# Two block sums of a weight matrix moved from VectorE to GpSimd, with two smaller moves beside them

## The chip, the cores and the metric

The kernel runs on one core of a Trainium2 chip. A core has five engines, each with its own instruction stream: TensorE (PE in the profile, with PEld for its weight loads), VectorE (DVE), ScalarE (ACT), GpSimd (POOL) and SyncE (SP), which here issues most of the DMAs. The engines run side by side and wait for each other through semaphores; each works through its own instructions in the order written. TensorE writes its results into PSUM, from where VectorE or ScalarE has to take them; POOL works on SBUF only in this kernel.

The metric is the device time of one execution in microseconds (us), the median of several runs. Lower is better.

## The reference

For each of 8 batches and 8 heads there is an `x` of 512 rows by 64 and a `state` of 32 rows by 64. Two attentions read from each other, and the rows of both results, with the heads side by side, pass through two layers with a leaky rectifier between them:

```python
scores = scale * np.matmul(x, state.transpose(0, 1, 3, 2))   # softmax over the 32 states -> a
xread = np.matmul(a, state)
scores2 = scale * np.matmul(state, x.transpose(0, 1, 3, 2))  # softmax over the 512 rows -> a2
sread = np.matmul(a2, x)
# rows of xread and sread of a batch: 512 + 32, each of 8 * 64 = 512 columns
h = x @ w_in                  # 512 -> 2048
g = np.maximum(0.01 * h, h)
out = g @ w_out               # 2048 -> 512
```

The output has 8 * 544 = 4352 rows of 512 float32.

## The kernel before, in words

**The first layer** of a batch isn't taken from `xread`. The kernel multiplies the batch's state by `w_in` first (`a_m`, matmuls of line 411, result `pm` in PSUM, copied to the tile `M`), and then `M` by the transposed softmax `aT` (`ff1`, line 432): two matmuls for each of 16 tiles of 128 hidden columns. ScalarE takes each result from PSUM through the rectifier into `hT` (line 437). Two PSUM banks of the tag "ph" take turns, so a tile's matmuls need the eviction of the tile two before it.

**The second layer** of batch 0 is written out in plain form (`piece`, line 537): four row tiles `i` of 128 rows, each 16 matmuls against the rows of `w_out_bf`, then a copy from PSUM into `ysb` and a store (`y_store`, lines 547 and 548). Row tiles 2 and 3 of batch 0 lie in one double PSUM bank, `wide` (`pyw` in the profile), with the tag "big"; tiles 0 and 1 in banks of the tag "py". The next user of "big" in TensorE's order is the `a_m` of batch 1's last quarter of `w_in`, in the step s = 3 of batch 1's first layer; it needs both copies out of `pyw`.

From batch 1's second half on, the second layer is made with seven block products instead of eight (a Winograd form). It needs four block sums of the weights, made once: `tw_sum(n, ...)`, line 576, with n = 1 to 4. Each is 8 row tiles by 256 columns:

```python
1: lambda: (w_block(0, 1, j0, j1), w_block(0, 0, j0, j1)),
2: lambda: (w_block(1, 1, j0, j1), tw[1][u][:, at]),
3: lambda: (w_block(1, 1, j0, j1), w_block(0, 1, j0, j1)),
4: lambda: (w_block(1, 0, j0, j1), tw[2][u][:, at]),
```

(first minus second in each; the fourth needs the second, the second needs the first). It also needs four block sums of `hT` for each batch: `s_sum` (line 597, tiles `S1` to `S4`) for whole batches, and `two_sum` (line 673, tiles `Sr`) for the second half of batch 1, whose state is `q1`. `two_product` (line 689, PSUM `ppr`) and `product` (line 632, `ppx` and `ppb`) are the matmuls of the seven products; product 7 uses the third block sum of the weights, product 4 the fourth, 5 and 6 the first and second. The additions of line 699 put two products together into `ysb` and free a PSUM bank.

**The order of work is written by hand.** All engines are scheduled manually: an engine does its instructions in the order in which the Python code issues them. Around the change this order is:

- a stretch ahead of batch 1's first layer (lines 992 to 1049): softmax of batch 1, the casts of x[2] and the cast of the states (`state_cast`, line 209, on POOL), the rest of batch 0's second layer, then `tw_sum(2)` on VectorE in two halves, `a_probs2(a0)` (two tiny operations, lines 345 and 347, and two scalings of 128x512, line 355, that finish batch 0's second softmax), `tw_sum(3)` on VectorE, and `cast_all(3)`, POOL's cast of x[3] to bfloat16 (line 132);
- batch 1's first layer (lines 1053 to 1095), s = 0 to 15. At s = 1 and 3 the last matmuls of batch 0's row tiles and their copies are issued; at s = 3 the scores of batch 2 (`a_scores(a2)`, line 256), the `a_m` into "big", and on VectorE `a_shift(a2)` (row maxima, line 266; spread, line 274; subtraction, line 280) and `a_max2` (line 331); ScalarE's exponential (line 284) follows at s = 7; at s = 9 VectorE makes the reciprocal and `aT` (lines 289 to 302) and `tw_sum(4)`;
- batch 2's first layer (line 1115 on), with the seven products of `q1` between its steps. At s = 0 VectorE makes the second halves (j = 4 to 7) of the sums 1 and 2 of `q1`, at s = 1, behind the shift of batch 3, the second half of sum 3; POOL makes sum 4, casts the other states and x[4].

SyncE's queue holds, in this order around the change: the load of x[3], four stores of batch 0's rows, eight small loads of states (line 203), the transpose of batch 3's x (line 234), which needs POOL's cast of x[3], then the transposes of the second softmaxes of batches 0 and 1.

Of the kernel before, what the change touches and what calls it, by code (L numbers as in the profile page):

```python
# [27 lines left out]
def kernel(  # L28
# [9 lines left out]
    nc = tc.nc  # L38
# [14 lines left out]
    VEC, SCA, POO = nc.vector.tensor_copy, nc.scalar.copy, nc.gpsimd.tensor_copy  # L53
# [261 lines left out]
    def a_shift(a):  # L315
        a_max(a)
        a_diff(a)

    def a_exp(a):
        a.e1 = block_exp(a.sh, NB)  # L320
# [230 lines left out]
    HJ = 8  # L551
# [12 lines left out]
    def w_block(r, c, j0, j1):  # L564
        return w_out_bf[:, HJ * r + j0:HJ * r + j1, HN * c:HN * (c + 1)]

    def tw_sum(n, j0, j1, eng):
        u, at = j0 // 4, slice(j0 % 4, j0 % 4 + j1 - j0)
        in0, in1 = {
# [4 lines that stand above are left out]
        }[n]()  # L574
        with nc.allow_low_precision(reason="operands of bf16 products"):
            eng.tensor_tensor(out=tw[n][u][:, at], in0=in0, in1=in1, op=ALU.subtract)  # L576
# [467 lines left out]
    for j in (0, 4):  # L1044
        tw_sum(2, j, j + 4, nc.vector)
    a_probs2(a0)
    for j in (0, 4):
        tw_sum(3, j, j + 4, nc.vector)
    cast_all(3)


# [3 lines left out]
    for s in range(16):  # L1055
        ff1(a1, h1, s)
        if s in (1, 3):
            two = ((2, SCA), (3, VEC)) if s == 1 else ((0, VEC), (1, SCA))
            for i, copy in two:
                piece(0, h0, i, 3, copy=None, js=half[1])  # L1060
            for i, copy in two:
                y_store(0, i, copy)
        elif s % 2:
            piece(*fill[s // 2 - 2])
        if s == 3:
            a_scores(a2)
            m_evict(a1, 3, a_m(a1, 3, "big"), SCA)
            a_shift(a2)
            a_max2(a2)
        elif s == 5:  # L1070
            load_state(1)
        elif s == 7:
            a_exp(a2)
            a_open(att_of[3], 3)
            a_xt_dma(att_of[3])
        elif s in (9, 11):
            a_exp2(a2, s // 2 - 4)
            if s == 9:
                a_a2t_pair(0, (0,))
                a_recip(a2)  # L1080
                a_probs(a2)
                for j in (0, 4):
                    tw_sum(4, j, j + 4, nc.vector)
            else:
                a_probs2(a2)
                load_x(4, nc.sync)
        elif s == 13:
            a_probs2(a1)
            a_a2t_pair(0, (1,))
            pm = [a_m(a2, 0, "big"), a_m(a2, 1, "sc")]  # L1090
            m_evict(a2, 0, pm[0], SCA)
            m_evict(a2, 1, pm[1], VEC)
            q1 = two_open(h1, 2 * P, ("S0", "S1"), "py")
            for n in (1, 2, 3):
                two_sum(q1, n, 0, 4, nc.vector)

# [16 lines left out]
    for b in range(2, B):  # L1115
        hT = hpool.tile([P, 16, S], BF16, name="hT", tag="hT")
        hTs[b] = hT
        a = att_of[b]
        nxt = att_of[b + 1] if b + 1 < B else None
        if b == 2:  # L1120
            two_keep(q1, "S2")
            fill = {i: [lambda i=i: piece(1, h1, i, 3)] for i in range(2)}
            for s, n in zip((2, 3, 5, 6, 8, 9, 11), (1, 2, 6, 5, 3, 7, 4)):
                fill[s] = [lambda n=n: two_product(q1, n)]
            fill[11].append(lambda: nc.sync.dma_start(pair_rows(1, 1), q1.y[:]))
        else:
            order = (2, 6, 5, 7, 3, 4)
            fill = {
                s: [lambda n=order[s // 2], v=s % 2: product(b - 1, n, v)] for s in range(12)
            }  # L1130
            for i, n in enumerate(order):
                if n not in (2, 7):
                    fill[2 * i + 1].append(lambda n=n: after(b - 1, n))
        fill[12 if b < 6 else 13] = [lambda: product(b, 1, 0)]
        fill[14] = [lambda: product(b, 1, 1, 0, 4)]
        fill[15] = [lambda: product(b, 1, 1, 4, 8), lambda: after(b, 1)]
        mid = MID.get(b, ())
        for s in range(16):
            ff1(a, hT, s)
            if mid and s == (1 if b == 2 else 2):  # L1140
                (o, c, tag), (o2, c2, tag2) = mid
                pm = a_m(att_of[o], c, tag)
                a_scores(nxt)
                m_spread(o2, c2, a_m(att_of[o2], c2, tag2))
                m_evict(att_of[o], c, pm, SCA)
                a_shift(nxt)
                if b > 2:
                    a_max2(nxt)
                else:
                    two_sum(q1, 3, 4, 8, nc.vector)  # L1150
            if s == 0:
                if b + 2 < B:
                    open_xb(b + 2)
                if b == 7:
                    a_a2t_pair(6)
                elif b != 6:
                    a_a2t(a)
                for n in (1, 2):
                    if b > 2:
                        s_sum(b - 1, n, 4, 8, nc.vector)  # L1160
                    else:
                        two_sum(q1, n, 4, 8, nc.vector)
            elif s == 1:
                if b > 2:
                    for j in range(0, HJ, 2):
                        s_sum(b - 1, 4, j, j + 2, nc.gpsimd)
                else:
                    for j in (4, 0):
                        two_sum(q1, 4, j, j + 4, nc.gpsimd)
                    state_cast(1, nc.gpsimd)  # L1170
                if b + 2 < B:
                    cast_all(b + 2)
            elif s == 4:
                if b == 2:
                    state_t(1)
                    a_sread(a0)
            elif s == 7:
                if b == 2:
                    a_sread(a1)
            elif s == 13:  # L1180
                if b < 6:
                    a_sread(a)
            elif s == 10:
                if b == 7:
                    a_sread(att_of[6])
            elif s == 12:
                if b == 7:
                    a_sread(a)
                for n in (1, 2):
                    s_sum(b, n, 0, 4, nc.vector)  # L1190
                for j in (0, 4):
                    s_sum(b, 3, j, j + 4, nc.vector)
            if nxt is not None:
                if s == 4 + bool(mid):
                    a_exp(nxt)
                elif s in ((6, 9) if b == 2 else (6, 7)):
                    if b == 2 and s == 6:
                        for f in fill.pop(6):
                            f()
                    a_exp2(nxt, int(s > 6))  # L1200
                if s == 7:
                    a_recip(nxt)
            if s == 9 and b + 2 < B:
                a_open(att_of[b + 2], b + 2)
                a_xt_dma(att_of[b + 2])
                if b + 3 < B:
                    load_x(b + 3, nc.sync)
            if b == 7:
                if s == 0:
                    fa_open()  # L1210
                elif s == 13:
                    fb_sums()
            for f in fill.get(s, ()):
                f()
            if b == 7 and s in FA_AT:
                i = FA_AT.index(s)
                fa_sum(i % 4 + 1, FJ * (i // 4), FJ * (i // 4 + 1))
            if s == 1:
                if b > 2:
                    after(b - 1, 2)  # L1220
            elif s == 3 and b == 2:
                a_max2(nxt)
            elif s == 7 and b > 2:
                after(b - 1, 7)
            if nxt is not None:
                if s == (8 if b == 2 else 7):
                    a_probs(nxt)
                elif s == 9:
                    a_probs2(nxt)
                elif s == 10:  # L1230
                    pms = [a_m(att_of[o], c, t) for o, c, t in END.get(b, ())]
                    for (o, c, t), pm in zip(END.get(b, ()), pms):
                        if t == "phpy":
                            m_spread(o, c, pm)
                        else:
                            m_evict(att_of[o], c, pm, VEC if t == "big" else SCA)
# [76 lines left out]
```

## Time and profile before

| | us |
|---|---|
| median of 3 runs (204.12 to 204.14) | 204.12 |
| the profiled execution | 203.73 |
| its span, first to last instruction | 202.0 |
| TensorE busy (matmuls) | 195.7 |
| VectorE busy | 162.1 |
| ScalarE busy | 141.8 |
| GpSimd busy | 63.4 |
| VectorE busy from 40 to 50 us | 9.67 |
| VectorE busy from 50 to 60 us | 9.79 |

In the timelines a line is: start, length, engine, line of the kernel, operation, output and inputs by the program's names, their shapes, and the number of instructions merged into it (x4). In brackets stands how long the engine was idle before and what it waited for. Start and length of a merged line are from its first start to its last end. The length of one VectorE or ScalarE instruction includes a tail in which the next one already runs: 0.69 us sums follow each other at 0.60. The ends of matmuls are modelled; the distance between their starts is the better measure: two matmuls of 512 columns take 0.43 us. The granted clock of TensorE is full in the whole profile.

### The profile page before, as it was taken

What the parts mean: (1) busy time and instruction counts of PE and PEld (TensorE: products, weight loads), DVE (VectorE), ACT (ScalarE), POOL (GpSimd) and SP (SyncE); (2) the same over time, 40 slices, a digit from 0 to 9 for tenths busy, and PEclk for the clock granted to TensorE, in tenths of its full rate; (3) what the DMA queues carried; (4) which work ended last, traced back from release to release, by engine and by line L of the source; (5) the groups of instructions that cost most, each with busy time, mean ns of one, the idle gap of its engine ahead of it and who ended that gap; (6) DMA issues with size and microseconds to landing.
All of it is one profiled execution on the core that took longest, in us unless ns stands there. A gap on an engine that the chain in (4) does not pass through costs nothing.

```text
span 202.0 us, 4620 instructions
## 1 busy us (share of the span) xinstructions
PE 195.7 (97%) x1880; PEld 130.0 (64%) x1880; DVE 162.1 (80%) x245; ACT 141.8 (70%) x272; POOL 63.4 (31%) x68
## 2 busy tenths in 40 slices
PE   7899999999989999999999999999999999999993
PEld 3643544444457667776776767676767777799982
DVE  2666797999999989974998889897999945984712
ACT  3679647889888868866787779686868555757420
POOL 8914181030280175017400670054004600540000
PEclk9999999999999999999999999999999999999999
DMA  5999999797999622953382505220025302210115
GB/s 197 212 207 298 209 290 154 165 344 151 246 219 200 229 52 43 247 229 60 61 248 109 159 3 104 105 107 0 0 86 166 63 3 97 114 43 12 52 40 170
DMA packets 38773, 27.75 MB, mean 137 GB/s; under 512 B 24416, under 2 KB 35808, under 8 KB 38752
## 3 DMA queue, kind: packets, MB, share of 16 engines
q1 hardware_dynamic: 33584, 20.78, 38.4%
q0 software_dynamic: 4832, 6.29, 15.3%
q10 hardware_dynamic: 336, 0.39, 0.7%
q8 instruction: 14, 0.23, 0.5%
q14 instruction: 7, 0.06, 0.1%
HBM read 17.30 MB, written 8.91 MB: 130 GB/s over the span
## 4 chain that ended last, share of the span: by engine, by line
PE 67%; DMA 15%; DVE 11%; POOL 3%; issue 1%; ACT 1%; ACTq 1%; POOLq 0%; DVEq 0%
PE ph L432 19%; PE ppx L632 18%; PE ppb L632 15%; DMA w_out_bf<-in_moe_w_out_dram 7%; DMA x<-in_x_dram 7%; PE ppr L689 5%; PE pf L510 3%; PE pm L411 3%; PE ppw L632 3%; DVE Sr L673 2%; POOL w_in_bf L145 2%; PE psr L384 2%; DVE tw L576 2%; DVE sh L274 1%; DVE mrow L266 1%
## 5 line engine op out<-in xcount | busy, mean ns | idle before, releaser
L437 ACT ACTIVATE hT<-ph 128x512 bf16<-128x512 f32 x112 | 66.6, 604 | 25.2 <-PE ph L432 24.3
L432 PE MATMUL ph<-aT,M 128*128 128x512 bf16 x224 | 65.3, 380 | 0.1
L597 POOL TENSOR_TENSOR S<-hT,S 128x512 bf16<-128x512 bf16 x24 | 31.9, 1348 | 84.5 <-DVE S L597 58.1
L632 PEld LDWEIGHTS <-S 128*128 128x128 bf16 x384 | 37.0, 98 | 12.7 <-issue 0.9
L632 PEld LDWEIGHTS <-hT 128*128 128x128 bf16 x288 | 28.0, 98 | 11.1
L597 DVE TENSOR_TENSOR S<-hT 128x1024 bf16<-128x1024 bf16 x24 | 24.1, 1031 | 4.4 <-ACT hT L437 4.4
L432 PEld LDWEIGHTS <-M 128*128 128x128 bf16 x224 | 20.9, 98 | 8.9 <-issue 3.0
L632 PE MATMUL ppx<-tw,S 128*128 128x256 bf16 x160 | 20.8, 273 | 0.0
L537 PEld LDWEIGHTS <-hT 128*128 128x128 bf16 x96 | 9.1, 98 | 11.4 <-issue 1.0
L537 PE MATMUL py<-w_out_bf,hT 128*128 128x512 bf16 x64 | 16.0, 379 | 0.0
L729 DVE TENSOR_TENSOR ysb<-ppb,s 128x512 f32<-128x512 f32 x12 | 8.3, 692 | 6.1 <-PE ppb L632 6.1
L132 POOL CAST xb<-xl 128x2048 bf16<-128x2048 f32 x5 | 9.5, 1890 | 9.8 <-DMA xl<-in_x_dram 9.8
L632 PE MATMUL ppb<-w_out_bf,hT 128*128 128x256 bf16 x96 | 12.4, 273 | 0.0
L632 PE MATMUL ppb<-tw,S 128*128 128x256 bf16 x96 | 12.4, 273 | 0.0
L632 PE MATMUL ppb<-w_out_bf,S 128*128 128x256 bf16 x96 | 12.3, 273 | 0.0
L425 ACT CAST M<-pm 128x1024 bf16<-128x1024 f32 x11 | 11.2, 1018 | 0.4 <-PE pm L411 0.4
L632 PE MATMUL ppx<-w_out_bf,hT 128*128 128x256 bf16 x80 | 11.2, 273 | 0.0
L337 ACT ACTIVATE e<-sc,mcol 128x512 bf16<-128x512 f32 x16 | 11.1, 698 | 0.0
L632 PE MATMUL ppx<-tw,hT 128*128 128x256 bf16 x80 | 10.4, 273 | 0.0
L331 DVE TENSOR_REDUCE mcol<-sc 128x2 f32<-128x1024 f32 x8 | 9.7, 1215 | 0.0
L284 ACT ACTIVATE e<-sh 128x1024 bf16<-128x1024 f32 x7 | 7.4, 1055 | 3.0 <-DVE sh L280 3.0
L266 DVE TRANSPOSE_TENSOR_REDUCE mrow<-sc 128x32 f32<-128x1024 f32 x7 | 8.7, 1243 | 0.5 <-PE sc L256 0.5
(148 smaller groups left out, 318.9 us busy)
## 6 DMA issues: line engine op xcount, KB each, us to landing
out_dram<-ysb SPq DMA_DIRECT2D x11, 512.0 KB, 2.6
xl<-in_x_dram SPq DMA_DIRECT2D x5, 1024.0 KB, 6.3
out_dram<-ysb SPq DMA_DIRECT2D x9, 256.0 KB, 4.6
w_in_bf<-in_moe_w_in_dram POOLq DMA_DIRECT2D x4, 512.0 KB, 9.0
xf<-in_x_dram SPq DMA_DIRECT2D x4, 256.0 KB, 3.7
w_out_bf<-in_moe_w_out_dram POOLq DMA_DIRECT2D x4, 256.0 KB, 14.2
x<-in_x_dram POOLq DMA_DIRECT2D x2, 512.0 KB, 13.8
w_out_bf<-in_moe_w_out_dram POOLq DMA_DIRECT2D x2, 512.0 KB, 16.5
```

Source lines behind the costliest of these rows:

```text
L132: nc.gpsimd.tensor_copy(xt[b][:].rearrange("p t h d -> p h t d"), xl[b][:].rearrange("p h (t d) -> p h t d", t=NT),)
L266: nc.vector.tensor_reduce(out=m1[:], in_=flat.rearrange("p (c j) -> p c j", j=NS), axis=AX.X, op=ALU.max, apply_transpose=True,)
L331: nc.vector.tensor_reduce(out=a.m2[:], in_=a.sc[:], axis=AX.X, op=ALU.max, negate=True)
L337: nc.scalar.activation(out=a.e2[:, g], in_=a.sc[:, g, :], func=AF.Exp, bias=a.m2[:, g:g + 1], accum_out=a.r2[:, g:g + 1],)
L425: copy(a.M[:, :, cols], pm[:])
L432: nc.tensor.matmul(ph[:], lhsT=a.M[:, g, P * j:P * (j + 1)], rhs=a.aT[:, g, :], start=(g == 0), stop=(g == 1),)
L437: nc.scalar.activation(out=hT[:, j, :], in_=ph[:], func=AF.Prelu, scale=1 / SCALE, alpha=0.01)
L537: nc.tensor.matmul(y.py, lhsT=hT[:, j, P * i:P * (i + 1)], rhs=w_out_bf[:, j, :], start=(j == 0), stop=(j == 15),)
L597: eng.tensor_tensor(out=part(n), in0=in0, in1=in1, op=op)
L632: nc.tensor.matmul(q[bank][v], lhsT=lhsT, rhs=w_of(n, j), start=q["open", bank] and j == 0, stop=j == 7, skip_group_check=True,)
L689: nc.tensor.matmul(q.bank[w], lhsT=lhsT, rhs=w_of(n, j), start=n in (1, 2, 5) and j == 0, stop=j == HJ - 1, skip_group_check=True,)
L729: nc.vector.tensor_tensor(out=to, in0=of, in1=in1, op=ALU.add)
```

## The change

Three parts, all in the written-out order; no operation is added or dropped.

1. The third and the fourth block sum of `w_out` are made by POOL (`nc.gpsimd`) in four pieces of two row tiles each, the fourth first, instead of by VectorE in two halves each. POOL does all eight pieces between its cast of the states and its cast of x[3]. On VectorE the third sum stood between `a_probs2(a0)` and the copies of batch 0's rows, the fourth behind `a_probs(a2)`.
2. The second half of sum 3 of `q1` (batch 1's tiles) is issued on VectorE at the end of the loop over batch 1's first layer, ahead of the second halves of sums 1 and 2, instead of behind the shift of batch 3 in batch 2's loop.
3. The copy of batch 0's row tile 0 out of PSUM is made by ScalarE instead of VectorE.

```diff
     for j in (0, 4):
         tw_sum(2, j, j + 4, nc.vector)
     a_probs2(a0)
-    for j in (0, 4):
-        tw_sum(3, j, j + 4, nc.vector)
+    for n in (4, 3):
+        for j in range(0, HJ, 2):
+            tw_sum(n, j, j + 2, nc.gpsimd)
     cast_all(3)
...
         if s in (1, 3):
-            two = ((2, SCA), (3, VEC)) if s == 1 else ((0, VEC), (1, SCA))
+            two = ((2, SCA), (3, VEC)) if s == 1 else ((0, SCA), (1, SCA))
...
                 a_recip(a2)
                 a_probs(a2)
-                for j in (0, 4):
-                    tw_sum(4, j, j + 4, nc.vector)
             else:
...
             q1 = two_open(h1, 2 * P, ("S0", "S1"), "py")
             for n in (1, 2, 3):
                 two_sum(q1, n, 0, 4, nc.vector)
+            two_sum(q1, 3, 4, 8, nc.vector)
...
                 if b > 2:
                     a_max2(nxt)
-                else:
-                    two_sum(q1, 3, 4, 8, nc.vector)
```

## The prediction

> **What bounds the kernel now.** I read the page first, then the chain of work over 33 to 62 us, where all parts of the change lie, then each engine's timeline there.
>
> ```profile
> span 202.0 us, 4620 instructions
> PE 195.7 (97%) x1880; PEld 130.0 (64%) x1880; DVE 162.1 (80%) x245; ACT 141.8 (70%) x272; POOL 63.4 (31%) x68
> ```
>
> TensorE is the bound on the average. But in this stretch the chain runs through VectorE (chain in order of time: start, length, what):
>
> ```profile
> 39.12 1.17 DVE mrow L266
> ...
> 42.91 1.06 ACT e L284
> ...
> 47.85 1.20 DVE tw L576 x2
> ...
> 58.18 1.92 DVE Sr L673
> 60.10 0.34 DVE ysb L699
> ...
> 60.49 1.05 PE ppr L689 x8
> ```
>
> Only from 60.49 on is it TensorE's. TensorE's timeline (start, length, work) gives what VectorE costs it:
>
> ```profile
> 38.44 0.41 PE L256 MATMUL sc<-xT,st_t 64*32 64x512 bf16 x8
> 38.66 0.40 PE L411 MATMUL pm<-w_in_bf,st 64*32 64x512 bf16 x8
> ...
> 42.48 1.03 PE L432 MATMUL ph<-aT,M 128*128 128x512 bf16 x4
> 43.34 1.03 PE L537 MATMUL py<-w_out_bf,hT 128*128 128x512 bf16 x4
> 44.50 1.08 PE L432 MATMUL ph<-aT,M 128*128 128x512 bf16 x4
> ...
> 52.44 0.40 PE L256 MATMUL sc<-xT,st_t 64*32 64x512 bf16 x8
> ...
> 53.87 0.59 PE L432 MATMUL ph<-aT,M 128*128 128x512 bf16 x2
> 54.62 1.03 PE L689 MATMUL ppr<-w_out_bf,hT 128*128 128x256 bf16 x8 [0.17 <-DVE M L1113]
> ...
> 59.00 0.59 PE L432 MATMUL ph<-aT,M 128*128 128x512 bf16 x2
> ```
>
> Four such matmuls start 0.86 apart from the next four (42.48 to 43.34), two take 0.43. So three holes can be read off: 43.34 + 0.86 = 44.20, but the next starts at 44.50 (0.30); 53.87 + 0.43 = 54.30 against 54.62 (0.32); 59.00 + 0.43 = 59.43 against 60.49 (1.06). A shorter VectorE can win back at most these 1.68 us; all other time here is matmul.
>
> **The change part by part.** VectorE's own rows:
>
> ```profile
> 33.52 0.69 DVE L576 TENSOR_TENSOR tw<-w_out_bf,tw 128x1024 bf16<-128x1024 bf16 x1
> 35.09 0.69 DVE L576 TENSOR_TENSOR tw<-w_out_bf,tw 128x1024 bf16<-128x1024 bf16 x1 [0.88 <-DMA w_out_bf<-in_moe_w_out_dram]
> 35.70 0.16 DVE L345 TENSOR_SCALAR r<-r 128x2 f32<-128x2 f32 x1
> ...
> 36.10 0.62 DVE L355 TENSOR_SCALAR a2p<-e,qc 128x512 bf16<-128x512 bf16 x2
> 36.63 1.29 DVE L576 TENSOR_TENSOR tw<-w_out_bf 128x1024 bf16<-128x1024 bf16 x2
> 37.83 0.69 DVE L547 COPY ysb<-pyw 128x512 f32<-128x512 f32 x1
> 38.43 0.69 DVE L547 COPY ysb<-py 128x512 f32<-128x512 f32 x1
> ...
> 57.04 1.22 DVE L280 TENSOR_TENSOR sh<-sc,sh 128x1024 f32<-128x1024 f32 x1
> ```
>
> Removed from VectorE: the third block sum (36.63 to 37.83, 1.20), the fourth (47.85, 1.20), and one copy (38.43 to about 39.03, 0.60). Moved: the half sum of Sr at 58.18, which takes 1.92 there.
>
> Added to POOL: eight 128x512 sums, between the state cast and the cast of x[3]. POOL's rows:
>
> ```profile
> 25.84 4.49 POOL L576 TENSOR_TENSOR tw<-w_out_bf 128x512 bf16<-128x512 bf16 x4 [4.36 <-DMA w_out_bf<-in_moe_w_out_dram]
> ...
> 32.52 0.86 POOL L209 TENSOR_SCALAR stb<-stf 128x256 bf16<-128x256 f32 x1 [2.18 <-DMA stf<-in_state_dram]
> 43.14 1.89 POOL L132 CAST xb<-xl 128x2048 bf16<-128x2048 f32 x1 [9.76 <-DMA xl<-in_x_dram]
> ...
> 57.93 1.89 POOL L132 CAST xb<-xl 128x2048 bf16<-128x2048 f32 x1
> ```
>
> Four such sums take 4.49, so 1.12 each in a row and 9.0 for eight. POOL's idle 9.76 ahead of the cast covers most of it. The first (tw4 from tw2) can start when VectorE's half of tw2 is done, 33.52 + 0.69, about 34.3.
>
> The price is what POOL does to VectorE. The half sum at 58.18 takes 1.92 beside the cast that ends at 57.93 + 1.89 = 59.82. Of its size elsewhere (minimum/median/maximum ns), and what happens when both engines sum (VectorE, then POOL, 154 to 157 us):
>
> ```profile
> L673 DVE TENSOR_TENSOR Sr<-hT x4: 415/418/1919, 52.0 to 58.2; 128x512 bf16<-128x512 bf16 x4
> ```
> ```profile
> L355 DVE TENSOR_SCALAR a2p<-e,qc x8: 347/353/354, 36.1 to 150.2; 128x512 bf16<-128x512 bf16 x8
> ```
> ```profile
> L576 POOL TENSOR_TENSOR tw<-w_out_bf x4: 1152/1154/1157, 25.8 to 29.2; 128x512 bf16<-128x512 bf16 x4
> ```
> ```profile
> 154.03 2.25 DVE L597 TENSOR_TENSOR S<-hT 128x1024 bf16<-128x1024 bf16 x2
> ```
> ```profile
> 154.28 1.44 POOL L597 TENSOR_TENSOR S<-hT,S 128x512 bf16<-128x512 bf16 x1 [14.66 <-DVE S L597]
> ```
> ```profile
> 155.69 1.59 POOL L597 TENSOR_TENSOR S<-hT,S 128x512 bf16<-128x512 bf16 x1
> ```
>
> They take turns: POOL's first ends at 155.72, VectorE's second at 156.28 (0.56 later), POOL's second at 157.28. Its own 1.15 taken off, POOL's second began near 156.13, just as VectorE ended. A VectorE sum that comes during a POOL sum waits for its end. The subtraction at 57.04, with one input in PSUM, keeps 1.22 beside POOL.
>
> Now the order after 34.3. POOL's first sum, with 0.15 allowed for the signal, runs 34.36 to 35.51. VectorE's second half of tw2 comes at 35.09, waits, ends 0.56 behind, at 36.07. POOL's second ends 1.56 behind its first, as above: 37.07. Behind it on VectorE stand the three scalings of batch 0 (one L345, two L355). No row shows a scaling beside POOL. Bounds for each: 0, and one POOL turn of 1.15. I take the upper end, since L355 is nearest to the rows that wait: bf16, SBUF only, 0.353 for 512 where the sum takes 0.418, whereas the row that doesn't wait is at the 1.22 per 1024 rate. L345 is like them but tiny, the least certain. Then, each scaling ending 0.1 to 0.25 behind a POOL sum and holding the next one up by 0.05 to 0.12 (from its length without the fixed part; the sums, longer, held it 0.41): L345 ends at 37.17, POOL's third at 38.27, the first L355 at 38.5, POOL's fourth at 39.54, the second L355 at 39.8. So the three scalings, over at 36.63 today, are over 3.2 later; less the 1.20 of the third block sum, the copy of pyw starts at 39.8 instead of 37.83 and ends near 40.45.
>
> Who waits for it: pyw lies in the bank "big", which TensorE's M matmuls at 38.66 write next. Today the copy ends at 37.83 + 0.69 = 38.52, only 0.14 ahead. So TensorE stops until 40.5, **1.84 lost**, with everything queued behind it. The row maximum (39.03 today) starts at about 40.4, so the exponential of ScalarE comes at 44.3 and TensorE's own 44.20 + 1.84 = 46.04 is later than what it waits for: the 0.30 hole closes, and it is 46.04 - 44.50 = **1.54 late**.
>
> From there VectorE catches up: it is late by about 1.4, less 1.20 (fourth sum gone), plus 0.34 (the Sr half sum in its new place, at the step of its neighbours, with POOL idle). It reaches the M copy before TensorE's matmuls, late by 1.54, have filled it, and TensorE doesn't wait for it any more: **0.32 back**. At 58.18 the 1.92 is gone; the addition into ysb runs at about 59.1 instead of 60.10, and TensorE is ready at 60.7: **1.06 back**. Sum: +1.84 - 0.30 - 0.32 - 1.06 = **+0.16**. Behind 60.49 the chain is TensorE's and keeps that offset.
>
> By the Trainium skill (SBUF — State Buffer, Who interferes with whom), a copy, cast or tensor_scalar in a two-port mode, and an operation with two SBUF inputs against a GpSimd one that reads SBUF, are blocked for the whole GpSimd instruction. No run here shows it for the scaling; by that rule all three wait, +0.16, and without it they cost 0 and the sum is that of the first rival.
>
> Edits at nothing. The copy on ScalarE:
>
> ```profile
> 38.54 0.58 ACT L547 COPY ysb<-py 128x512 f32<-128x512 f32 x1 [0.15 <-PE py L537]
> 39.13 1.01 ACT L425 CAST M<-pm 128x1024 bf16<-128x1024 f32 x1
> ```
>
> It starts in the 0.15 idle, so M's cast would be 0.24 later; here that cast waits for TensorE to about 41.0 anyway. Without that cover the next exponential waits for VectorE (42.91), so still at most 0.1.
> SyncE's queue:
>
> ```profile
> 40.31 5.86 SPq L203 DMA_DIRECT2D stf<-in_state_dram  x8
> 46.28 1.77 SPq L234 DMA_TRANSPOSE xT<-xb  x1
> ```
> ```profile
> xT<-xb SPq DMA_TRANSPOSE x1, 4.4
> ```
>
> The store of pyw stands ahead of these and waits for the late copy: all of it moves by some 1.6 to 2, the transpose to about 48.3, landing (4.4) at 52.7. POOL's cast of x[3] ends at 39.54 + four sums of 1.15 + 1.89 = 46.0, ahead of that. The scores of batch 3 (52.44 today) then start at 52.44 + 1.54 = 53.98: hidden with 1.3 to spare; beyond it TensorE waits one for one.
>
> **The rivals.**
> *None of the scalings waits* (for: no row shows it; against: their rate). Then the copy of pyw is on time, the maxima start when the scores are there (38.44 + 0.41 = 38.85 instead of 39.03): -0.1, and both later holes close: -0.1 - 0.32 - 1.06 = -1.5, **202.6**.
> *Only the two L355 wait*, L345 being too small. One turn less: the copy ends at 39.25, TensorE loses 0.64; 0.64 - 0.30 - 1.38 = -1.04, **203.1**.
> *VectorE loses one more turn* and it is slower: the reciprocal between the scalings waits too, or POOL's next sum is let in ahead of a waiting scaling. For it: POOL always has its next sum queued. Against: at 154 us VectorE got in between two. One turn is 1.15 on the copy of pyw and on TensorE at once, with no hole left: +0.16 + 1.15 = 1.3, **205.4**. It decides from a copy that ends 0.3 later than 40.45.
> The Trainium skill (Vector Engine (DVE) Microarchitecture Reference, 5.1 Performance modes) lists copy, cast and tensor_scalar for the two-port modes and no reciprocal; no run here shows it.
>
> **How the numbers follow.** The profiled execution took 203.73 (span 202.0 and 1.73 around it), 0.39 under the median of 204.12; I put the differences on the median. No change within what can be told is 0.2%, 0.41 us. Forecast +0.16: 204.3, chance 0.50; its own range is 203.9 to 204.9 (each turn 1.12 to 1.35, the transpose a little late). No scaling waits 0.16; only L355 0.12; one more turn 0.14; 0.08 for what I don't see. Of the forecast's half, 0.35 lies within 0.41 of before, 0.12 above and 0.03 below. Faster: 0.16 + 0.12 + 0.03 + 0.03 = 0.34; same 0.35; slower 0.12 + 0.14 + 0.05 = 0.31. The range reaches down to the first rival and leaves the slow one out: 202.5 to 205.0.
>
> **What would show it.** Right: L345 and L355 behind the second tw2 half stretched to about 1 us each, alternating with POOL's sums; the copy of pyw ending near 40.4; TensorE's M matmuls waiting for it; the holes at 44.5, 54.6 and 60.5 gone. Wrong: scalings of 0.16 and 0.35 beside POOL and M matmuls at 38.7 (first rival); a fourth stretch (third); or scores of batch 3 waiting for their transpose.

## The result: 0.2% faster, and where TensorE stands now

The changed kernel takes 203.46 us (median of 13 runs, 202.95 to 203.75) against 203.90 for the kernel before beside it (13 runs): a ratio of 0.9977, 95% interval 0.9967 to 0.9986. That is 0.44 us faster. The forecast was 204.3, no change that could be told; the measured time lies in the wide range, outside the forecast's own range of 203.9 to 204.9, and on the other side of "before". The forecast stood on 204.12 for the kernel before, from three runs; on 203.90 it would have been 204.06, so 0.22 of the 0.84 between forecast and result is the base. In three of the experiments one execution ran longer at a lower granted clock (206.40 to 208.50 us); the medians below include it, the ratios do not.

The profiled execution took 203.55, its span is 201.8. VectorE's timeline after, at the place where the prediction put the cost (start, length, work, idle before):

```profile
33.68 0.68 DVE L576 TENSOR_TENSOR tw<-w_out_bf,tw 128x1024 bf16<-128x1024 bf16 x1
34.87 1.27 DVE L576 TENSOR_TENSOR tw<-w_out_bf,tw 128x1024 bf16<-128x1024 bf16 x1 [0.51 <-DMA w_out_bf<-in_moe_w_out_dram]
36.06 1.11 DVE L345 TENSOR_SCALAR r<-r 128x2 f32<-128x2 f32 x1
37.21 0.17 DVE L347 RECIPROCAL qc<-r 128x2 f32<-128x2 f32 x1
37.41 2.17 DVE L355 TENSOR_SCALAR a2p<-e,qc 128x512 bf16<-128x512 bf16 x2
39.50 0.68 DVE L547 COPY ysb<-pyw 128x512 f32<-128x512 f32 x1
...
58.68 0.41 DVE L699 TENSOR_TENSOR ysb<-ppr,rkept 128x256 f32<-128x256 f32 x1
```

The scaling of two elements, 0.16 before, lasts 1.11; the two of 512, together 0.62 before, last 2.17. Nothing in brackets stands behind them: the wait shows as length only. POOL's sums one by one in the same stretch, and the first of the two L355 by itself:

```profile
35.55 1.60 POOL L576 TENSOR_TENSOR tw<-w_out_bf,tw 128x512 bf16<-128x512 bf16 x1
```
```profile
37.11 1.15 POOL L576 TENSOR_TENSOR tw<-w_out_bf,tw 128x512 bf16<-128x512 bf16 x1
```
```profile
37.41 1.00 DVE L355 TENSOR_SCALAR a2p<-e,qc 128x512 bf16<-128x512 bf16 x1
```
```profile
38.23 1.21 POOL L576 TENSOR_TENSOR tw<-w_out_bf,tw 128x512 bf16<-128x512 bf16 x1
```

L345 ends at 37.17, POOL's second sum at 37.15. The first L355 ends at 38.41, POOL's third at 38.26. The second ends at 39.58, POOL's fourth at 39.44. They take turns, each VectorE operation right behind a POOL sum. The reciprocal keeps its 0.17 while POOL's third sum runs. TensorE's timeline after:

```profile
37.64 1.03 PE L537 MATMUL py<-w_out_bf,hT 128*128 128x512 bf16 x4
38.72 0.41 PE L256 MATMUL sc<-xT,st_t 64*32 64x512 bf16 x8
40.23 0.41 PE L411 MATMUL pm<-w_in_bf,st 64*32 64x512 bf16 x8 [1.10 <-DVE ysb L547]
...
44.92 1.03 PE L537 MATMUL py<-w_out_bf,hT 128*128 128x512 bf16 x4
45.78 1.03 PE L432 MATMUL ph<-aT,M 128*128 128x512 bf16 x4
...
55.09 0.59 PE L432 MATMUL ph<-aT,M 128*128 128x512 bf16 x2
55.52 1.04 PE L689 MATMUL ppr<-w_out_bf,hT 128*128 128x256 bf16 x8
...
59.90 0.59 PE L432 MATMUL ph<-aT,M 128*128 128x512 bf16 x2
60.33 1.04 PE L689 MATMUL ppr<-tw,Sr 128*128 128x256 bf16 x8
```

The M matmuls wait for the copy of pyw, as forecast. The three holes are gone: 44.92 + 0.86 = 45.78, 55.09 + 0.43 = 55.52, 59.90 + 0.43 = 60.33, each exactly where the next work starts. One stall has taken the place of three.

To put sizes on it, the two executions are laid over each other at the group of matmuls just ahead, which in the kernel before is

```profile
37.48 1.03 PE L537 MATMUL py<-w_out_bf,hT 128*128 128x512 bf16 x4
```

| distance from that group to | before | after | difference | forecast |
|---|---|---|---|---|
| the M matmuls (38.66 / 40.23) | 1.18 | 2.59 | +1.41 | +1.84 |
| the first layer's tile behind the hole at 44.5 (44.50 / 45.78) | 7.02 | 8.14 | +1.12 | +1.54 |
| the product behind the hole at 60.5 (60.49 / 60.33) | 23.01 | 22.69 | -0.32 | +0.16 |

A second profile of the changed kernel, taken with the last experiments, gives the same three distances: 2.59, 8.14 and 22.69. Of the kernel before there is one profile only.

The chain that ended last changes accordingly. Over 33 to 63 us it leaves VectorE for good at the copy of pyw:

```profile
39.58 0.61 DVE ysb L547
40.19 0.04 issue
40.23 0.41 PE pm L411 x8
```

From there on it is all TensorE's, where before it came back to VectorE until 60.49.

### The profile page after: what moved, and what is told of

The parts are those of the page before. It is cut to its first block, busy times and chain, and to the rows that moved or that the text cites. A ratio compares the mean times of both kernels' runs of the same rounds, so it can differ in the third digit from the quotient of the medians.

```text
span 201.8 us, 4599 instructions
## 1 busy us (share of the span) xinstructions
PE 193.9 (96%) x1853; PEld 129.9 (64%) x1880; DVE 161.8 (80%) x240; ACT 142.0 (70%) x273; POOL 72.7 (36%) x76
## 4 chain that ended last, share of the span: by engine, by line
PE 76%; DMA 15%; POOL 3%; DVE 3%; issue 1%; ACTq 1%; ACT 0%; POOLq 0%; DVEq 0%
PE ph L432 21%; PE ppx L632 18%; PE ppb L632 15%; DMA x<-in_x_dram 7%; DMA w_out_bf<-in_moe_w_out_dram 7%; PE ppr L689 6%; PE pm L411 3%; PE py L537 3%; PE pf L510 3%; PE ppw L632 3%; PE psr L384 2%; POOL w_in_bf L145 2%; DVE a2p L355 1%; DMA out_dram<-ysb 1%; DVE tw L576 1%
## 5 line engine op out<-in xcount | busy, mean ns | idle before, releaser
L432 PE MATMUL ph<-aT,M 128*128 128x512 bf16 x202 | 60.6, 379 | 0.1
L597 DVE TENSOR_TENSOR S<-hT 128x1024 bf16<-128x1024 bf16 x24 | 24.8, 1056 | 3.6 <-ACT hT L437 3.5
L576 POOL TENSOR_TENSOR tw<-w_out_bf 128x512 bf16<-128x512 bf16 x8 | 9.0, 1161 | 4.0 <-DMA w_out_bf<-in_moe_w_out_dram 4.0
L289 DVE TRANSPOSE_TENSOR_REDUCE r<-e 128x32 f32<-128x1024 bf16 x7 | 8.7, 1245 | 1.0 <-ACT e L284 0.7
```

What stands on the lines that cost most here:

```text
L289: nc.vector.tensor_reduce(out=r1[:], in_=e1[:].rearrange("p (c j) -> p c j", j=NS), axis=AX.X, op=ALU.add, apply_transpose=True,)
L432: nc.tensor.matmul(ph[:], lhsT=a.M[:, g, P * j:P * (j + 1)], rhs=a.aT[:, g, :], start=(g == 0), stop=(g == 1),)
L597: eng.tensor_tensor(out=part(n), in0=in0, in1=in1, op=op)
```

## The experiments

Two theories stood against each other at first: *turns* (each VectorE scaling waits for one POOL sum, the copy of pyw is late, TensorE stands), and rivals by which the stall or the gain came from elsewhere. Diffs are against the changed kernel unless the text says otherwise. Each ratio is to the kernel before, run on the same chip, with a 95% interval.

**The scalings ahead of POOL's start.**

```diff
-    for j in (0, 4):
-        tw_sum(2, j, j + 4, nc.vector)
     a_probs2(a0)
+    for j in (0, 4):
+        tw_sum(2, j, j + 4, nc.vector)
     for n in (4, 3):
```

> The changed kernel with VectorE's scalings of batch 0 (lines 345 to 355) issued ahead of the second block sum of w_out, so that they are done before POOL has its first sum. Theory (turns): the changed kernel's three scalings wait for POOL's sums, the copy of pyw is late and TensorE stands 1.3 us at its M matmuls. Without that the copy of pyw starts near 37.9, the M matmuls near 38.9, and the time is 0.7 to 1.4 under the changed kernel's 203.46: 202.1 to 202.8. It stays at the upper end if line 293, also a scaling, now falls beside POOL's cast of x[3] and waits (about 1 us more on VectorE, 0.3 on TensorE). Rival (the stall has another cause, such as the transposed states or the banks): the M matmuls still start near 40.2 and the time stays within 0.3 of 203.46.

Measured: 202.93, ratio 0.9947 (0.9935 to 0.9959), a little above the range for *turns* and 0.5 under the changed kernel; the rival is out. VectorE, then POOL, then TensorE:

```profile
33.82 0.16 DVE L345 TENSOR_SCALAR r<-r 128x2 f32<-128x2 f32 x1
...
45.48 1.22 DVE L293 TENSOR_SCALAR r<-r 128x32 f32<-128x32 f32 x1
```
```profile
44.78 1.89 POOL L132 CAST xb<-xl 128x2048 bf16<-128x2048 f32 x1
```
```profile
38.97 0.40 PE L411 MATMUL pm<-w_in_bf,st 64*32 64x512 bf16 x8
...
55.00 1.03 PE L689 MATMUL ppr<-w_out_bf,hT 128*128 128x256 bf16 x8 [0.34 <-DVE M L1113]
```

The scalings are back at 0.16 and the M matmuls start at 38.97: the stall is gone. But POOL, which now starts its sums later (35.51 instead of 34.44), is still casting x[3] when line 293 comes; that scaling of 32 elements takes 1.22 instead of 0.18 and ends at 46.70, 0.03 behind the cast. VectorE is late again, and TensorE stands before the product at 55.0. Part of what was won is given back there.

**Half the length of a turn.**

```diff
     for n in (4, 3):
-        for j in range(0, HJ, 2):
-            tw_sum(n, j, j + 2, nc.gpsimd)
+        for j in range(HJ):
+            tw_sum(n, j, j + 1, nc.gpsimd)
```

> The changed kernel with POOL's eight sums of 128x512 cut to sixteen of 128x256, the same work. Theory (turns): each wait of a scaling is one POOL sum, so it halves, to about 0.55 us; the copy of pyw starts near 38.0 and TensorE hardly stands: 202.1 to 202.8. Rival (VectorE is slowed by POOL's total work, not by the length of a turn): the three scalings take as long together as in the changed kernel (3.3 us) and the time stays within 0.3 of 203.46.

Measured: 203.07, ratio 0.9953 (0.9940 to 0.9966).

```profile
35.37 0.63 DVE L345 TENSOR_SCALAR r<-r 128x2 f32<-128x2 f32 x1
...
36.23 1.19 DVE L355 TENSOR_SCALAR a2p<-e,qc 128x512 bf16<-128x512 bf16 x2
...
45.16 1.56 DVE L293 TENSOR_SCALAR r<-r 128x32 f32<-128x32 f32 x1
```

The lengths nearly halve with the piece: 1.11 to 0.63 and 2.17 to 1.19, with the same elements summed on POOL. That is a wait for one instruction, not a share of POOL's total work. The M matmuls start at 38.65, without a stall. The time missed its range by 0.3, for the same reason as with the scalings first: the sixteen pieces end later, the cast starts at 44.80 instead of 43.88, line 293 lasts 1.56, and TensorE stands 0.85 before the product at 55.02.

**Twice the length of a turn.**

```diff
     for n in (4, 3):
-        for j in range(0, HJ, 2):
-            tw_sum(n, j, j + 2, nc.gpsimd)
+        for j in (0, 4):
+            tw_sum(n, j, j + 4, nc.gpsimd)
```

> The changed kernel with POOL's sums in four of 128x1024. Theory (turns): a turn is about 2.25 us; the second half of tw2 waits about 1.8, both scalings of line 355 wait a whole turn, the copy of pyw ends near 42.8 and TensorE's M matmuls start near 42.9 instead of 40.2: 206.1, between 205.3 and 206.8. Rival (total work counts): within 0.3 of 203.46.

Measured: 205.52, ratio 1.0069 (1.0052 to 1.0086), slower than before and 2.06 above the changed kernel.

```profile
36.99 0.15 DVE L345 TENSOR_SCALAR r<-r 128x2 f32<-128x2 f32 x1
...
37.38 4.16 DVE L355 TENSOR_SCALAR a2p<-e,qc 128x512 bf16<-128x512 bf16 x2
```
```profile
37.15 2.12 POOL L576 TENSOR_TENSOR tw<-w_out_bf,tw 128x1024 bf16<-128x1024 bf16 x1 [0.63 <-DVE r L345]
```
```profile
42.19 0.41 PE L411 MATMUL pm<-w_in_bf,st 64*32 64x512 bf16 x8 [3.09 <-DVE ysb L547]
```

The two L355 take 4.16, nearly twice 2.17. L345 slipped through: POOL's second sum needs the second half of tw2, which ended only at 37.07, and started at 37.15, when L345 was over. The M matmuls start 1.96 later than in the changed kernel, nearly all of the 2.06: here no hole is left to absorb a stall.

**Only the moved half sum of Sr, in the kernel before.**

```diff
             for n in (1, 2, 3):
                 two_sum(q1, n, 0, 4, nc.vector)
+            two_sum(q1, 3, 4, 8, nc.vector)
...
-                else:
-                    two_sum(q1, 3, 4, 8, nc.vector)
```

> The kernel before with only the second part: the second half of sum 3 of batch 1's tiles put ahead. Theory (the sum is hidden from POOL's cast and costs 0.34 where it took 1.92): the hole of TensorE at 60.5 (1.06) goes, the one at 54.6 grows by 0.34: 0.7 under before, 203.2 if before is at 203.9; so this part alone is worth more than the whole change. Rival (the hole at 60.5 goes only because VectorE has lost the block sums too): within 0.2 of before.

Measured: 203.10, ratio 0.9956 (0.9943 to 0.9969), 0.9 under before. TensorE:

```profile
53.83 0.59 PE L432 MATMUL ph<-aT,M 128*128 128x512 bf16 x2
54.94 1.03 PE L689 MATMUL ppr<-w_out_bf,hT 128*128 128x256 bf16 x8 [0.51 <-DVE M L1114]
...
59.31 0.59 PE L432 MATMUL ph<-aT,M 128*128 128x512 bf16 x2
59.75 1.04 PE L689 MATMUL ppr<-tw,Sr 128*128 128x256 bf16 x8
```

The product that stood until 60.49 starts at 59.75; the hole ahead of it has closed (59.31 + 0.43 = 59.74), the one at 54.6 has grown by about the sum's 0.34 (53.83 + 0.43 = 54.26 against 54.94, so 0.68 instead of 0.32). This part alone is worth more than the whole change.

**Only the sums on POOL.** The changed kernel without its second and third part.

```diff
-            two_sum(q1, 3, 4, 8, nc.vector)
...
                 if b > 2:
                     a_max2(nxt)
+                else:
+                    two_sum(q1, 3, 4, 8, nc.vector)
...
-            two = ((2, SCA), (3, VEC)) if s == 1 else ((0, SCA), (1, SCA))
+            two = ((2, SCA), (3, VEC)) if s == 1 else ((0, VEC), (1, SCA))
```

> The kernel before with only the first part: block sums 3 and 4 of w_out on POOL. Theory (the sums on POOL cost TensorE's stand at the M matmuls and give VectorE time that is worth less): pyw late as in the changed kernel, and the copy of row tile 0, on VectorE again, pushes the row maxima back by 0.6, TensorE by another 0.3 to 0.4; the holes at 54.6 and 60.5 go, since TensorE comes late. The changed kernel plus 0.3: within 0.4 of before. Rival (the sums are what made the change faster): 0.4 or more under before.

Measured: 204.20, ratio 0.9999 (0.9984 to 1.0014): nothing. TensorE:

```profile
40.49 0.41 PE L411 MATMUL pm<-w_in_bf,st 64*32 64x512 bf16 x8 [1.23 <-DVE ysb L547]
...
45.17 1.03 PE L537 MATMUL py<-w_out_bf,hT 128*128 128x512 bf16 x4
46.42 1.08 PE L432 MATMUL ph<-aT,M 128*128 128x512 bf16 x4 [0.22 <-ACT hT L437]
```

Two stalls are there: the one for pyw, and behind ScalarE the hole that the kernel before has at 44.5, here 45.17 + 0.86 = 46.03 against 46.42 (0.39 instead of 0.30). ScalarE's exponential waits for VectorE, which had one more copy to make than in the changed kernel. What the sums take off VectorE is paid for by TensorE.

**The changed kernel with the Sr half sum back in its old place.**

```diff
-            two_sum(q1, 3, 4, 8, nc.vector)
...
                 if b > 2:
                     a_max2(nxt)
+                else:
+                    two_sum(q1, 3, 4, 8, nc.vector)
```

> The changed kernel with the half sum of Sr back in its old place. Theory: TensorE's late M matmuls alone have closed the hole at 60.5, so the moved sum gives nothing here as long as it comes just ahead of POOL's cast of x[4] (58.7 against 58.8 in the changed kernel): within 0.2 of the changed kernel, 203.3 to 203.7. If the cast comes first, the sum waits for it, 1.9 us as before, and TensorE stands about 1 at 60.5: 204.5. Rival (the gain of the whole change is that of the moved sum, 0.9 as alone, and the rest loses 0.5): 204.3 to 204.5 without such a wait.

Measured: 203.55, ratio 0.9976 (0.9954 to 0.9997), the same as the changed kernel. VectorE, then POOL:

```profile
58.69 0.41 DVE L673 TENSOR_TENSOR Sr<-hT 128x512 bf16<-128x512 bf16 x1
```
```profile
58.83 2.02 POOL L132 CAST xb<-xl 128x2048 bf16<-128x2048 f32 x1 [1.12 <-PE psr L384]
```

So the moved sum, worth 0.9 alone, is worth nothing once the sums are on POOL. The cast of x[4] now waits for TensorE's late matmuls of line 384 and comes 0.14 behind the half sum instead of 0.25 ahead of it. The same hole has been paid for by the earlier stall.

This version differs from the one with only the sums on POOL in the copy of row tile 0 alone, and both ran on one chip. TensorE's timeline at the place where that one stands 0.39:

```profile
44.92 1.03 PE L537 MATMUL py<-w_out_bf,hT 128*128 128x512 bf16 x4
45.78 1.03 PE L432 MATMUL ph<-aT,M 128*128 128x512 bf16 x4
```

There is no hole (44.92 + 0.86 = 45.78). So beside the sums on POOL the copy on ScalarE is worth about 0.4 by the traces and 0.65 by the medians (204.20 against 203.55), though the intervals of the two ratios still overlap. What the changed kernel gains on the kernel before is about this much.

**A version built on these readings.** The scalings first, then the third sum on VectorE, in time in which VectorE otherwise stands idle (1.71 ahead of the copy of pyw in the version with the scalings first), then the second; POOL makes only the fourth.

```diff
-    for j in (0, 4):
-        tw_sum(2, j, j + 4, nc.vector)
     a_probs2(a0)
-    for n in (4, 3):
-        for j in range(0, HJ, 2):
-            tw_sum(n, j, j + 2, nc.gpsimd)
+    for j in (0, 4):
+        tw_sum(3, j, j + 4, nc.vector)
+    for j in (0, 4):
+        tw_sum(2, j, j + 4, nc.vector)
+    for j in range(0, HJ, 2):
+        tw_sum(4, j, j + 2, nc.gpsimd)
     cast_all(3)
```

> A version built on the readings so far: the changed kernel with the scalings of batch 0 first, then the third block sum on VectorE again, in the time in which it otherwise waits for TensorE, then the second; POOL makes only the fourth (four pieces) and so is done before its cast of x[3] can start. Theory: no scaling falls beside POOL (those of lines 345 and 355 are over before, line 293 comes after the cast), pyw on time, the fourth sum off VectorE's chain: the holes at 54.6 and 60.5 both gone, 1.4 to 1.6 under before, some 0.4 under the version with scalings first alone (202.93). Rival (what is left is not VectorE's): the same as that version, within 0.15.

Measured: 202.50, ratio 0.9929 (0.9916 to 0.9942): 1.5 under before, 1.0 under the changed kernel. POOL, VectorE, TensorE:

```profile
36.60 4.87 POOL L576 TENSOR_TENSOR tw<-w_out_bf,tw 128x512 bf16<-128x512 bf16 x4 [3.29 <-DVE tw L576]
43.67 1.89 POOL L132 CAST xb<-xl 128x2048 bf16<-128x2048 f32 x1 [2.21 <-DMA xl<-in_x_dram]
```
```profile
45.21 0.39 DVE L293 TENSOR_SCALAR r<-r 128x32 f32<-128x32 f32 x1
```
```profile
38.70 0.40 PE L411 MATMUL pm<-w_in_bf,st 64*32 64x512 bf16 x8
...
54.23 1.04 PE L689 MATMUL ppr<-w_out_bf,hT 128*128 128x256 bf16 x8
...
59.05 1.04 PE L689 MATMUL ppr<-tw,Sr 128*128 128x256 bf16 x8
```

No stall at pyw, no holes at 54 and 59. POOL waits for x[3] again, so its cast starts as early as the load lets it; line 293 still loses 0.2, because that cast ends only at 45.56.

**All but the sums.** The changed kernel with block sums 3 and 4 on VectorE as before, run twice, the second time on one chip with the changed kernel.

```diff
-    for n in (4, 3):
-        for j in range(0, HJ, 2):
-            tw_sum(n, j, j + 2, nc.gpsimd)
+    for j in (0, 4):
+        tw_sum(3, j, j + 4, nc.vector)
     cast_all(3)
...
                 a_recip(a2)
                 a_probs(a2)
+                for j in (0, 4):
+                    tw_sum(4, j, j + 4, nc.vector)
```

> The changed kernel without its first part: block sums 3 and 4 on VectorE as before, the half sum of Sr ahead, the copy of row tile 0 on ScalarE. Theory (the sums on POOL are a loss here): 0.9 to 1.1 under before, so 0.4 to 0.6 faster than the whole change; the copy adds at most 0.15 to the moved sum alone, since the row maxima then wait for the scores. Rival (all three parts are needed): no faster than the whole change.

Measured: 203.36, ratio 0.9970 (0.9952 to 0.9987); its interval overlaps the changed kernel's, so the two were put on one chip:

> The changed kernel as it is, on one chip with the next, since the two were so far compared only through the kernel before. Theory (its sums on POOL are a loss as placed): 0.4 to 0.6 above the next kernel. Rival (the intervals of the two overlap because they are the same): within 0.2.

> The changed kernel without its first part (block sums 3 and 4 on VectorE as before), beside the changed kernel itself: 0.4 to 0.6 under it, about 203.0 if before is at 203.9.

Measured: the changed kernel 203.49, ratio 0.9971 (0.9952 to 0.9989); without the sums 203.00, ratio 0.9941 (0.9918 to 0.9964). The medians are 0.49 apart, as the theory has it. The intervals of the two ratios touch, but they carry the spread of the kernel before as well; set side by side, all seven runs without the sums (202.75 to 203.30) lie under all twelve with them (203.34 to 204.06). That the sums on POOL cost about 0.5 rests on this and on the profiles' spans (201.2 and 201.5 without the sums, 201.8 with them). The copy on ScalarE wasn't run alone; with the sums on VectorE no gain of it beyond the moved sum can be seen (203.00 and 203.36 against 203.10).

## Why the prediction was right and wrong

- **The mechanism was right.** The scalings wait for POOL's sums, the copy of pyw is late, TensorE's M matmuls stand, the three holes close. The pieces of half and of double length settle it: the wait follows the length of one POOL instruction.
- **The step that failed is a size: "1.84 lost".** It measured 1.41. The copy of pyw was put 5.44 behind the start of POOL's first sum (34.36 to 39.8); it came 5.06 behind (34.44 to 39.50). I let the scalings end 0.10, 0.23 and 0.26 behind a POOL sum; they end 0.02, 0.15 and 0.14 behind. I let them hold up POOL more than they do: its second to fourth sum end over 2.29 (37.15 to 39.44), not 2.47. And I started the copy at the end of the last scaling, while it starts 0.08 before, as VectorE's instructions overlap at their tails. Some 0.1 more is that TensorE itself came later in this execution (37.64 against 37.48), while POOL's first sum came 0.08 later than I had put it, so less of their delay reached it.
- **That size decided the sign.** The sum was a difference of large terms: a stall of 1.84 against 1.68 of holes. With 1.41 the same working gives 1.41 - 0.30 - 0.32 - 1.06 = -0.27; the overlay shows -0.32, the medians -0.44. The last 0.1 isn't explained; the two profiled executions themselves are only 0.18 apart (203.73 and 203.55), since TensorE came to this place 0.16 later in the second.
- **The holes given back were right in size**: by the overlay 1.41 - 1.12 = 0.29 of the first, and 1.12 + 0.32 = 1.44 of the other two, where 0.30 and 1.38 were forecast. The reason given for the 1.06, that the half sum no longer stands at 58.18, isn't needed: with the half sum back there the hole stays closed, because TensorE's late matmuls hold the cast of x[4] back until the half sum has begun.
- **"Three scalings wait" was right, also for the tiny one** (1.11 for two elements). By the Trainium skill (SBUF — State Buffer, Who interferes with whom) a tensor_scalar in a two-port mode is blocked for the whole of a GpSimd instruction that was issued first; the trace agrees, 1.11 and 1.00 where 0.16 and 0.35 are normal, though no run here shows the mode. The third rival did not occur: the reciprocal took 0.17 beside a POOL sum, and VectorE got in after each of POOL's first four.
- **SyncE's queue was wrong without harm.** I had the transpose of batch 3's x move from 46.28 to 48.3. It starts at 46.37:

```profile
41.63 4.63 SPq L203 DMA_DIRECT2D stf<-in_state_dram  x8
46.37 1.67 SPq L234 DMA_TRANSPOSE xT<-xb  x1
```

  The eight loads start 1.3 late but take 4.63 instead of 5.86.
- **What the prediction did not look at**: what each part is worth without the others. The moved half sum alone gives 0.9, the sums on POOL alone nothing, and the first is worth nothing on top of the second. The copy on ScalarE, to which the prediction gave no gain of its own, is the part that pays beside the sums on POOL (about 0.4 by the traces).

## What to carry to other kernels

In these runs work moved from VectorE to POOL was free only beside VectorE operations that read PSUM (the copy of 0.68, the row maxima of 1.23) or that are a transpose, a reduction or a reciprocal in SBUF (1.25, 1.25 and 0.17); without POOL the same operations take within 0.02 of that. A scaling or a two-input sum in SBUF, however small, waited for the end of POOL's instruction. So keep POOL's pieces short, or put such operations ahead of them. Look at what the delayed engine copies out of PSUM next: here the cost arrived at TensorE there. When a forecast is the difference of a stall and the holes that it closes, an error of a few tenths in the stall turns the sign, and the chances should say so; try each part alone, since parts that close the same hole don't add up.

## What the runs showed that was not expected

A scaling of two elements per partition can last 1.11 us, and one of 32 elements 1.56, only because of when it is issued. The profile names no wait for it: the operation is just long. The only sign is its minimum elsewhere (0.16 and 0.18) and a POOL instruction that ends where it ends. And such a wait moves with small shifts: line 293 was free in the changed kernel (0.18), took 1.22 when POOL's work started 1.1 us later, and 0.39 with half of that work gone: the cast then had to wait for x[3] to land and ended at 45.56, while line 293 came at 45.21.
